# The operands of the float32r products of a Fourier and feed-forward kernel, laid out in two pools of their own at multiples of 256 bytes

## The chip, the cores and the metric

The kernel runs on one core of one Trainium2 chip. The metric is the device time of one execution in microseconds (us), median of several runs. The engines are named as in the profile: PE is TensorE's matmul, PEld its loading of weights, DVE is VectorE, ACT is ScalarE, POOL is GpSimd, SP is SyncE, which here issues DMAs.

## The reference

```python
# x: 8 x 3136 x 256 float32
X = np.fft.fft(x, axis=1); X = np.fft.fft(X, axis=2)
x = X.real.astype(np.float32)                      # real part of a 2-D Fourier transform
mu, var = mean(x, -1), mean((x - mu) ** 2, -1)
xn = (x - mu) / np.sqrt(var + 1e-06) * g_ln        # layer norm with a gain
out = x + np.maximum(xn @ w_ch1, 0.0) @ w_ch2      # 256 -> 1024 -> 256, and the residual
```

## The kernel before, in words

The transform along the sequence is done in two steps of small matrix products, with a store to a scratch tensor in DRAM and a load in another order between them (`step1`, `store1`, `relayout`, `step2`). The transform along the 256 features is folded into the first weight matrix, so that the 49 chunks of 256 tokens (`c` = 0 to 48) go from `step2` straight into the feed-forward part. Rows k and N-k of the transform are mirror images, so that one chunk stands for 512 output rows.

Nearly all work of PE is in the feed-forward part. It runs in 392 steps, `s = 8 * c + f`, where `f` is one of eight slices of 128 of the 1024 hidden features. A product of two float32 numbers is made of three float32r products, high times low, low times high and high times high (`PASSES`), so every operand exists as a pair of tiles `..._hi` and `..._lo`:

- `moe1_a(s)` (L345): six products. The weights, 128 x 128, come from `w1_hi` and `w1_lo`; the moving operand, 128 x 256, is one half (`j` = 0 or 1) of the chunk's tiles `ckl` and `ckh` (tags `ck_lo`, `ck_hi`). The two results go to a PSUM tile `ab`; ACT copies one of them (`asb`, L350), and DVE forms sum and difference in `h` (L351, L352).
- `moe1_b(s)` (L359, L360): ACT writes `h_hi` from `h` through a relu, DVE writes `h_lo`.
- `moe2(s)` (L395): twelve products. The weights are the four 128-column pieces of `h_lo` and `h_hi`, the moving operand is the slice `f` of `w2_hi` and `w2_lo`, 128 x 256; they accumulate in PSUM tiles `acc`.

`tc.manual_schedule` keeps the order in which the program issues on every engine. The main loop issues `moe1_b(s-1)`, `moe1_a(s)`, then `moe2(s-3)`; the dictionaries `late` and `after` insert the rest by step number: the next batch's transform (`fold_zw`, `fold_eo`, `fold_hi`, `fold_lo`, then `step1` with the float32r products of `t1_hi`, `t1_lo` and the tiles `fh`, `fl`, L254), `step2` (plain float32 products, L301, whose `l` part writes `ckl` on DVE at L325), the residual (plain float32 products of the tile `ck`, L419), statistics, `finish` and `store_out`. At the start the weights arrive as 64-bit floats and are turned into float32 pairs by `convert_*`, `finish_*`, `transform_w1`, `round_w1`, `split_w2`; these borrow the buffers of tags `f_hi`, `f_lo`, `h`, `h_lo`, `zw` and `s2`.

All tiles in SBUF are in two pools, `const` (one buffer each) and `work` (as many buffers as a tag's `bufs`, used in turn). Buffers follow one another in the order of first use, each at a multiple of 32 bytes, so the sizes set the addresses. The tags `ck`, `ck_hi`, `ck_lo` and `h_hi` (which `fold_zw` borrows for a tile of 2 x 264 floats) have buffers of 2112 bytes a partition, 64 bytes over a multiple of 256; `h_lo`, `f_hi` and `f_lo` have 2048. In the compiled program the starts of the float32r operands are these, modulo 256:

| operand | role | start modulo 256 |
|---|---|---|
| `w1_hi`, `w1_lo` (pieces 512 bytes apart) | weights of L345 | 224 |
| `ckh`, first half, in chunks c mod 3 = 0, 1, 2 | moving of L345 | 224, 96, 32 |
| `ckl`, first half, in chunks c mod 3 = 0, 1, 2 | moving of L345 | 160, 32, 224 |
| second half of `ckh` and `ckl` | moving of L345 | 32 more than the first |
| `w2_hi`, `w2_lo` (slices 1024 bytes apart) | moving of L395 | 224 |
| `h_lo` (pieces 512 bytes apart) | weights of L395 | 32 |
| `h_hi` in steps f mod 4 = 0, 1, 2, 3 (pieces 512 bytes apart) | weights of L395 | 96, 32, 224, 160 |
| `fh`, `fl` | moving of L254 | 32 |
| `t1_hi`, `t1_lo` | weights of L254 | 160 |

So in the steps with odd `f` the weights of L395 lie at 32 and 32, or 32 and 160; in those with even `f` at 32 and 96, or 32 and 224. The last buffer ends at byte 224,736 of a partition.

## Time and profile before

| | |
|---|---|
| median of 3 runs | 1017.01 us (1016.2 to 1017.36) |
| profiled execution, span | 1015.8 us, granted TensorE clock 1.000 |
| from that span to the median of the runs | 1.2 us |
| PE busy | 1005.0 us, 99% of the span, 8288 matmuls |
| DVE, ACT, POOL busy | 814.4, 541.2, 244.3 us |
| chain that ended last | PE 91%, of it L395 50% and L345 25% |

The profile lists no time of the profiled execution other than its span, so 1015.8 us stands beside the runs as it is; what lies around the span is at most the 1.2 us of the difference. Matmuls overlap in the array: one lasts about 280 ns in the records, and the next starts some 115 ns later. What a product costs the kernel is therefore read from the distance between starts, or from the chain, which lists a group of products with the time that it took of the chain, not from the mean duration.

### The profile page before, as it was taken

What the parts mean: (1) busy time and instruction counts of PE and PEld (TensorE: products, weight loads), DVE (VectorE), ACT (ScalarE), POOL (GpSimd) and SP (SyncE); (2) the same over time, 40 slices, a digit from 0 to 9 for tenths busy, and PEclk for the clock granted to TensorE, in tenths of its full rate; (3) what the DMA queues carried; (4) which work ended last, traced back from release to release, by engine and by line L of the source; (5) the groups of instructions that cost most, each with busy time, mean ns of one, the idle gap of its engine ahead of it and who ended that gap; (6) DMA issues with size and microseconds to landing.
All of it is one profiled execution on the core that took longest, in us unless ns stands there. A gap on an engine that the chain in (4) does not pass through costs nothing.

```text
span 1015.8 us, 21769 instructions
## 1 busy us (share of the span) xinstructions
PE 1005.0 (99%) x8288; PEld 983.7 (97%) x8289; DVE 814.4 (80%) x2190; ACT 541.2 (53%) x1416; POOL 244.3 (24%) x278
## 2 busy tenths in 40 slices
PE   9999999999999999999999999999999999999998
PEld 6799999999999999999999999999999999999998
DVE  7688887878787787878877887878788788788887
ACT  3655556554555555655556545554555554455453
POOL 2146413520153203441044301532034300000000
PEclk9999999999999999999999999999999999999999
DMA  9934243233122511333132232224101230100101
GB/s 349 262 135 136 74 148 103 84 91 107 53 94 84 156 43 53 103 118 104 44 114 95 73 105 74 83 95 134 45 32 43 73 104 23 43 22 22 43 22 43
DMA packets 41528, 92.10 MB, mean 91 GB/s; under 512 B 4176, under 2 KB 18704, under 8 KB 40528
## 3 DMA queue, kind: packets, MB, share of 16 engines
q1 hardware_dynamic: 40016, 88.87, 27.0%
q8 instruction: 66, 1.08, 0.5%
q0 software_dynamic: 320, 1.05, 0.3%
q10 hardware_dynamic: 1088, 0.79, 0.2%
q14 instruction: 38, 0.31, 0.1%
HBM read 50.32 MB, written 40.37 MB: 89 GB/s over the span
## 4 chain that ended last, share of the span: by engine, by line
PE 91%; DVE 5%; ACT 2%; DMA 1%; issue 1%; SPq 0%; DVEq 0%; ACTq 0%
PE acc L395 50%; PE ab L345 25%; PE ps L301 5%; PE psy L419 4%; PE ps L254 3%; DVE h_lo L360 2%; DVE h L351 1%; DVE h L352 1%; ACT h_hi L359 1%; PE ps L247 1%; PE ps L249 1%; PE pw L659 1%; DMA scratch<-s 1%; DMA s<-scratch 1%; ACT asb L350 0%
## 5 line engine op out<-in xcount | busy, mean ns | idle before, releaser
L395 PE MATMUL acc<-w_hi,h_hi 128*128 128x256 f32 x1568 | 438.6, 280 | 0.0
L395 PE MATMUL acc<-w_hi,h_lo 128*128 128x256 f32 x1568 | 438.4, 280 | 0.1
L395 PE MATMUL acc<-w_lo,h_hi 128*128 128x256 f32 x1568 | 438.4, 280 | 0.0
L360 DVE SCALAR_TENSOR_TENSOR h_lo<-h,h_hi 128x512 fp32r<-128x512 f32 x392 | 288.1, 735 | 168.8 <-ACT h_hi L359 166.9
L359 ACT ACTIVATE h_hi<-h 128x512 fp32r<-128x512 f32 x392 | 250.3, 639 | 266.8 <-DVE h L352 266.6
L395 PEld LDWEIGHTS acc<-w_hi,h_lo 128*128 128x128 f32 x1568 | 295.3, 188 | 0.5 <-DVE h_lo L360 0.4
L395 PEld LDWEIGHTS acc<-w_lo,h_hi 128*128 128x128 f32 x1568 | 295.0, 188 | 0.0
L395 PEld LDWEIGHTS acc<-w_hi,h_hi 128*128 128x128 f32 x1568 | 295.0, 188 | 0.0
L345 PE MATMUL ab<-ckl,w_hi 128*128 128x256 f32 x768 | 221.0, 288 | 2.7 <-DVE h L352 2.5
L345 PE MATMUL ab<-ckh,w_lo 128*128 128x256 f32 x768 | 216.2, 281 | 0.5 <-ACT ckh L321 0.3
L345 PE MATMUL ab<-ckh,w_hi 128*128 128x256 f32 x768 | 214.9, 280 | 0.0
L217 POOL TENSOR_TENSOR fl<-f,fh 128x512 fp32r<-128x512 f32 x49 | 64.7, 1321 | 502.0 <-ACT fh L211 495.7
L351 DVE TENSOR_TENSOR h<-asb,ab 128x256 f32<-128x256 f32 x384 | 158.8, 414 | 1.5 <-ACT asb L350 1.5
L352 DVE TENSOR_TENSOR h<-asb,ab 128x256 f32<-128x256 f32 x384 | 158.9, 414 | 0.0
L345 PEld LDWEIGHTS ab<-ckl,w_hi 128*128 128x128 f32 x768 | 144.5, 188 | 6.9 <-issue 2.8
L350 ACT COPY asb<-ab 128x256 f32<-128x256 f32 x384 | 139.4, 363 | 18.1 <-PE ab L345 12.5
L345 PEld LDWEIGHTS ab<-ckh,w_lo 128*128 128x128 f32 x768 | 145.0, 189 | 2.9 <-ACT ckh L321 0.5
L345 PEld LDWEIGHTS ab<-ckh,w_hi 128*128 128x128 f32 x768 | 145.1, 189 | 0.0
L321 ACT CAST ckh<-ps 128x392 fp32r<-128x392 f32 (+49 forms) x112 | 39.7, 356 | 65.5 <-PE ps L301 65.3
L257 ACT COPY s<-ps 128x508 f32<-128x508 f32 x56 | 32.7, 585 | 73.1 <-PE ps L254 60.1
L301 PE MATMUL ps<-tab_s,s 112*128 112x98 f32 (+1 forms) x512 | 65.6, 273 | 0.7 <-DMA s<-scratch 0.7
L301 PEld LDWEIGHTS ps<-tab_s,s 112*128 112x128 f32 x512 | 62.1, 192 | 1.2 <-PE pw L659 1.2
(108 smaller groups left out, 963.9 us busy)
## 6 DMA issues: line engine op xcount, KB each, us to landing
xs<-x SPq DMA_DIRECT2D x56, 512.0 KB, 4.6
out<-o SPq DMA_DIRECT2D x96, 256.0 KB, 3.1
scratch<-s SPq DMA_DIRECT2D x49, 256.0 KB, 2.2
s<-scratch SPq DMA_DIRECT2D x7, 1792.0 KB, 10.2
w1p_all<-w SPq DMA_DIRECT2D x8, 512.0 KB, 8.9
scratch<-s POOLq DMA_DIRECT2D x4, 256.0 KB, 6.4
s<-scratch SPq DMA_DIRECT2D x2, 448.0 KB, 5.8
s<-scratch SPq DMA_DIRECT2D x1, 896.0 KB, 12.3
```

The costliest lines, as they stand in the source:

```text
L217: nc.gpsimd.tensor_tensor(out=lo, in0=f, in1=hi.bitcast(F32), op=ALU.subtract)
L257: nc.scalar.copy(s[:, :, :, :127], ps[:, :, :, :127])
L301: nc.tensor.matmul(ps[:, h, k0 - base:k1 - base], s2[b][:KP, g, 128 * h:128 * h + 128], tab_s[:, h, k0:k1], start=(h == 0 and g == 2 * j), ...
L321: nc.scalar.copy(hi, src)
L345: nc.tensor.matmul(pt, wt[wi][:, j, fs], ch[xi][:, j, :w], start=(n == 0), stop=(n == 2))
L350: nc.scalar.copy(asb[:, :w], pa)
L351: nc.vector.tensor_tensor(out=h[:, :w], in0=asb[:, :w], in1=pb, op=ALU.add)
L352: nc.vector.tensor_tensor(out=h[:, w:], in0=asb[:, :m], in1=pb[:, :m], op=ALU.subtract)
L359: nc.scalar.activation(h_hi, h, AF.Relu)
L360: nc.vector.scalar_tensor_tensor(out=h_lo, in0=h, scalar=0.0, in1=h_hi.bitcast(F32), op0=ALU.max, op1=ALU.subtract)
L395: nc.tensor.matmul(acc[c, i][:, side], hs[xi][:, h0:h0 + 128], ws[wi][:, f], start=(f == 0 and side == 0 and n == 0), stop=(f == 7 and n = ...
L419: nc.tensor.matmul(ps[:, j, :129 + j], ck[:, j], ty_s[:, j, :129 + j], start=(j == 0), stop=True, skip_group_check=True)
```

## The change: two pools, and sizes that are multiples of 256 bytes

Two pools are opened ahead of `const`. `moving` holds `w2_hi`, `w2_lo`, and the tags `f_hi`, `f_lo`, `ck_hi`, `ck_lo`; an unused tile of 128 bytes at its start (`margin`) brings the first operand from byte 16,512 to 16,640, which is 65 times 256. `weights` holds `w1_hi`, `w1_lo`, `t1_hi`, `t1_lo`, and the tags `ck`, `h_hi`, `h_lo` and `s2`. The widths of `ck_hi` and `ck_lo` grow from 264 to 320 columns a half (a half is then 1280 bytes), of `ck` to 288, of `h_hi` to 576 floats (2304 bytes); the products still read the same columns. `zw` loses its unused columns. Every start in the table above becomes 0 modulo 256. Six buffers grow by 448 bytes, three by 192, four by 192, three shrink by 64, and with the margin the last buffer ends 3,968 bytes later, at 228,704. Numbers of buffers, instructions, their order on each engine and their shapes stay. Tiles that stay in `const` and `work` move to other addresses as well.

```diff
+CKW = 320
+HW = 576
...
 def tile_kernel(ctx: ExitStack, tc: tile.TileContext, x, g_ln, w1, w2, tu, tab, tz, ty, tw, out):
     nc = tc.nc
+    moving = ctx.enter_context(tc.tile_pool(name="moving", bufs=1))
+    weights = ctx.enter_context(tc.tile_pool(name="weights", bufs=1))
     const = ctx.enter_context(tc.tile_pool(name="const", bufs=1))
     work = ctx.enter_context(tc.tile_pool(name="work", bufs=2))
...
+    moving.tile([128, 32], F32, name="margin")
+    w2_hi = moving.tile([128, 8, D], F32R, name="w2_hi")
+    w2_lo = moving.tile([128, 8, D], F32R, name="w2_lo")
+    w1_hi = weights.tile([128, 2, FF], F32R, name="w1_hi")
+    w1_lo = weights.tile([128, 2, FF], F32R, name="w1_lo")
+    t1_hi = weights.tile([128, 128], F32R, name="t1_hi")
+    t1_lo = weights.tile([128, 128], F32R, name="t1_lo")
...
-    t1_hi = const.tile([128, 128], F32R, name="t1_hi")
...
-    w2_lo = const.tile([128, 8, D], F32R, name="w2_lo")
...
     def fold_zw(b, i, eng):
-        t = work.tile([128, 2, MAXW], F32, tag="h_hi" if i > 3 and b == 0 else "zw",
-                      name=f"zw{b}_{i}", bufs=4 if i > 3 and b == 0 else 3)
-        z, w = (t[:, h, :256].rearrange("p (s d) -> p s d", s=2) for h in range(2))
+        if i > 3 and b == 0:
+            t = weights.tile([128, HW], F32, tag="h_hi", name=f"zw{b}_{i}", bufs=4)
+        else:
+            t = work.tile([128, 2 * 256], F32, tag="zw", name=f"zw{b}_{i}", bufs=3)
+        z, w = (t[:, 256 * h:256 * h + 256].rearrange("p (s d) -> p s d", s=2) for h in range(2))
...
-        hi = work.tile([128, 2, 2, 128], F32R, tag="f_hi", name=f"fh{b}_{i}")
+        hi = moving.tile([128, 2, 2, 128], F32R, tag="f_hi", name=f"fh{b}_{i}", bufs=2)
...
-        lo = work.tile([128, 2, 2, 128], F32R, tag="f_lo", name=f"fl{b}_{i}")
+        lo = moving.tile([128, 2, 2, 128], F32R, tag="f_lo", name=f"fl{b}_{i}", bufs=2)
...
-            s2[b] = work.tile([128, 16, D], F32, tag="s2", name=f"s2_{b}")
+            s2[b] = weights.tile([128, 16, D], F32, tag="s2", name=f"s2_{b}", bufs=2)
...
-                chunk[c] = (work.tile([128, 2, MAXW], F32, tag="ck", name=f"ck{c}", bufs=3),
-                            work.tile([128, 2, MAXW], F32R, tag="ck_hi", name=f"ckh{c}", bufs=3),
-                            work.tile([128, 2, MAXW], F32R, tag="ck_lo", name=f"ckl{c}", bufs=3))
+                parts = (weights.tile([128, 2, CKW - 32], F32, tag="ck", name=f"ck{c}", bufs=3),
+                         moving.tile([128, 2, CKW], F32R, tag="ck_hi", name=f"ckh{c}", bufs=3),
+                         moving.tile([128, 2, CKW], F32R, tag="ck_lo", name=f"ckl{c}", bufs=3))
+                chunk[c] = tuple(p[:, :, :MAXW] for p in parts)
...
-        h_hi = work.tile([128, n], F32R, tag="h_hi", name=f"h_hi{s}", bufs=4)
-        h_lo = work.tile([128, n], F32R, tag="h_lo", name=f"h_lo{s}", bufs=4)
+        h_hi = weights.tile([128, HW], F32R, tag="h_hi", name=f"h_hi{s}", bufs=4)[:, :n]
+        h_lo = weights.tile([128, n], F32R, tag="h_lo", name=f"h_lo{s}", bufs=4)
```

In the conversion of the weights at the start, `convert_e`, `convert_m` and `w1p_all` take their buffers from the pools in which the tags now are, with the same numbers of buffers.

## The prediction, made before the changed kernel was run

> **What bounds the kernel now.** I read the page first: its summary, the share of each line in the chain, and the costliest groups.

> ```profile
> span 1015.8 us, 21769 instructions
> PE 1005.0 (99%) x8288; PEld 983.7 (97%) x8289; DVE 814.4 (80%) x2190; ACT 541.2 (53%) x1416; POOL 244.3 (24%) x278
> PEclk9999999999999999999999999999999999999999
> ...
> PE acc L395 50%; PE ab L345 25%; PE ps L301 5%; PE psy L419 4%; PE ps L254 3%; DVE h_lo L360 2%; DVE h L351 1%; DVE h L352 1%; ACT h_hi L359 1%; PE ps L247 1%; PE ps L249 1%; PE pw L659 1%; DMA scratch<-s 1%; DMA s<-scratch 1%; ACT asb L350 0%
> ...
> L395 PE MATMUL acc<-w_hi,h_hi 128*128 128x256 f32 x1568 | 438.6, 280 | 0.0
> ...
> L360 DVE SCALAR_TENSOR_TENSOR h_lo<-h,h_hi 128x512 fp32r<-128x512 f32 x392 | 288.1, 735 | 168.8 <-ACT h_hi L359 166.9
> ...
> L345 PE MATMUL ab<-ckl,w_hi 128*128 128x256 f32 x768 | 221.0, 288 | 2.7 <-DVE h L352 2.5
> ```

> PE is busy for 99% of the span at a full granted clock. Its two large lines have three passes each, of which one row stands here: 3 x 1568 = 4704 products at L395 and 3 x 768 = 2304 at L345. The last column says how long PE stood idle before them: 0.0 and 2.7 us. So the 7008 products of 256 columns set the time, and only the distance between their starts can move it: any nanosecond on each is 7.0 us. The durations of 280 ns overlap and say nothing of the distance. I took that from the chain in order of time, which merges the products of a group (start, length in us, what).

> ```profile
> 471.87 1.76 PE ps L301 x16
> 473.63 0.92 PE psy L419 x8
> 474.55 0.72 PE ab L345 x6
> 475.27 1.38 PE acc L395 x12
> 476.65 0.71 PE ab L345 x6
> 477.36 1.41 PE acc L395 x12
> 478.76 0.70 PE ab L345 x6
> 479.46 1.36 PE acc L395 x12
> 480.82 0.70 PE ab L345 x6
> 481.52 1.42 PE acc L395 x12
> 482.94 0.70 PE ab L345 x6
> 483.64 1.38 PE acc L395 x12
> 485.02 0.70 PE ab L345 x6
> 485.72 1.43 PE acc L395 x12
> ```

> The groups of twelve at L395 are the steps with f = 3, 4, 5, 6, 7, 0. The same twelve products, on the same engine with nothing to wait for, take 1.38, 1.41, 1.36, 1.42, 1.38, 1.43 us: 115, 118, 113, 118, 115, 119 ns a product. The odd steps are the short ones. What differs between odd and even steps is where `h_hi` lies: at 32 or 160 modulo 256 in the odd ones, at 96 or 224 in the even ones; `w2` is at 224 and `h_lo` at 32 in all. `moe1_a` takes 0.70 to 0.72 us for six, 117 to 120 ns. The timeline shows how the step of 1.36 us runs (start, duration); its first two products are left out.

> ```profile
> 479.52 0.28 PE L395 MATMUL acc<-w_hi,h_hi 128*128 128x256 f32 x1
> ...
> 480.54 0.28 PE L395 MATMUL acc<-w_hi,h_hi 128*128 128x256 f32 x1
> ```

> Nine distances: 1.02 / 9 = 113.3 ns, all of them 0.11 or 0.12 us in the timeline; after two or three products the distance has settled. Is it another engine that disturbs PE in the slow groups? Near the end there is a stretch with DVE and ACT idle.

> ```profile
> 1010.66 0.48 DVE L482 SCALAR_TENSOR_TENSOR o<-acc,r,y 128x256 f32<-128x256 f32 x1 [0.16 <-PE acc L395]
> ...
> 1011.03 0.28 PE L395 MATMUL acc<-w_hi,h_lo 128*128 128x256 f32 x1
> 1011.03 0.19 PEld L395 LDWEIGHTS acc<-w_lo,h_hi 128*128 128x128 f32 x1
> ...
> 1011.50 0.28 PE L395 MATMUL acc<-w_lo,h_hi 128*128 128x256 f32 x1
> ...
> 1011.58 0.48 DVE L482 SCALAR_TENSOR_TENSOR o<-acc,r,y 128x256 f32<-128x256 f32 x1 [0.43 <-PE acc L395]
> ```

> Four distances in 0.47 us are 117.5 ns, though DVE ended at 1011.14 and began again at 1011.58, and no other engine computes in between. So the slow pace is PE's own. The weight load at 1011.03 shows what runs beside each product: the loading of the next product's weights starts with it, so two streams read SBUF at once, 1024 bytes a partition moving and 512 bytes of weights. That two streams of one engine hinder each other by where they lie is my reading; the rows show only that pace goes with the address.

> **The change part by part.** Instructions, order, waits and numbers of buffers stay, so no step is moved past a queue and no wait is added. What remains are addresses.

> *Base.* From the groups above: L395 takes 1.38 in odd and 1.42 in even steps, mean 1.40 / 12 = 116.7 ns; L345 0.705 / 6 = 117.5 ns. Weighted by 4704 and 2304 that is 117.0 ns, and 7008 x 117.0 = 820 us of the 1015.8.

> *Products of 256 columns.* After the change both streams start at 0 modulo 256 in every step, which no step shows now. Ends of the bound: the shortest distance that any PE group of this kernel keeps between weight loads is L301's, 1.76 / 16 = 110 ns, in which products of only 98 columns wait for their weights; it would give 7008 x 7.0 = 49 us less. The longest group is 1.43 / 12 = 119.2 ns; everywhere it would give 7008 x 2.2 = 15 us more. Which value? In the odd steps with f mod 4 = 1 all weights lie alike (32), and the pace settles; in the even steps the two kinds of weights lie differently (32 against 96 or 224) and it stays long. The change makes all weights and all moving operands alike, in L345 too, so I take the settled pace of the step at 479.52, 113.3 ns, for nine tenths of the products and 118 for the rest (the first few after a residual or a `step2`, which are plain float32 and start the pattern anew): 0.9 x 113.3 + 0.1 x 118 = 113.8 ns. That is 7008 x 3.2 = 22.4 us less.

> [...]

> *Products of 512 columns.* L254 has 3 x 49 = 147.

> ```profile
> 420.26 0.39 PE L254 MATMUL ps<-fl,t_hi 128*128 128x512 f32 x1
> ...
> 420.96 0.28 PE L345 MATMUL ab<-ckl,w_hi 128*128 128x256 f32 x1
> ```

> From the first of three to the product that follows them, 0.70 / 3 = 233 ns each. The same ratio (113.8 / 117.0) would make it 227: 147 x 6 = 0.9 us less. Ends: 220 (110 x 2) and 238, 1.9 us less to 0.7 more.

> *Plain float32 products* (L301, L419) move too: `ck` and `s2` are now in `weights`. L301 takes 110 ns by its weight loads, L419 0.92 / 8 = 115 ns. I take zero; with 512 and 400 of them, a nanosecond is 0.9 us in all.

> *DVE, ACT, POOL.* Their tiles change addresses as well. DVE's `h_lo` takes 735 ns in the mean; DVE has 814 us of work in a span that would still be 993 us, 82%, and its work is covered by PE. If that cover went, the price is the view's own: L345 waits for L352 2.5 us now, by the last column of its row. A PE that is 2% faster shortens the slack of the three steps by which `moe2` lags `moe1_a` by 0.1 us or so; I take 0.5 us of new waits, ends 0 and 3 (the 2.5 of now once more).

> *DMA.* Destinations move, sizes do not; zero, as DMAs end few waits of PE (the chain has 2% for them).

> Sum: -22.4 - 0.9 + 0.5 = -22.8 us. Against the profiled span, 1015.8 - 22.8 = 993.0; the median of the runs lies 1.2 us above the span, so 994 us.

> **The rivals.**

> *Alignment locks in the slow pace (slower).* In the even steps `h_hi` at 96 or 224 is a multiple of 128 away from `w2` at 224, and exactly these steps are slow; in odd steps it is 64 away modulo 128, and these are fast. If what counts is that both streams start in the same place modulo 128, then the change puts every step in the slow class. Price: 118.5 ns (1.42 / 12 = 118.3, and L345 at 117 to 120) instead of 117.0, 7008 x 1.5 = 10.5 us more, 1027 us; with 119.2 everywhere 1032. It decides if the settled pace exceeds 117.0 ns. For it: the rows above. Against it: in L345 the weights are always at 224, the moving halves in chunk 21 at 224, 0, 160 and 192, in chunk 22 at 96, 128, 32 and 64, and the groups (chunk 22 from the row at 478.76 on) take 0.70 to 0.71 us in both, so the difference alone does not make the pace there. Chance 0.28.

> *Nothing low in the address matters.* The settled pace may come from higher bits or from the state in which a group begins: the step at 468.33 (f = 1, same residues as the one at 479.46) takes 1.41 us.

> ```profile
> 468.33 1.41 PE acc L395 x12
> ```

> Then the new addresses are another draw, and the mean stays at 117.0 within half a nanosecond, 3.5 us: 1013 to 1021 us, middle 1017. This is also the case in which the change does not do what it says. [...] Chance 0.22.

> *More than the settled pace.* If being aligned removes the excess altogether, PE falls to the pace of weight loads, 110 ns: 968 us; half way, 980. No step shows it. Chance 0.08, counted with the gain.

> **How the numbers follow.** Settled pace, 985 to 1008 us: 0.42, the likeliest, and its middle is the forecast, 994. Better than that, 968 to 985: 0.08. Another draw, 1013 to 1021: 0.22, of which 0.07 faster, 0.10 within, 0.05 slower. Slow lock, 1019 to 1034: 0.28, of which 0.02 within. A change of 0.2%, 2 us, is about what a measurement of this kernel can tell from none. Faster: 0.42 + 0.08 + 0.07 = 0.57; same 0.12; slower 0.05 + 0.26 = 0.31. For the range I leave out the best part of the gains (below 979) and the upper part of the slow case (above 1028): 979 to 1028. The likeliest case alone has 985 to 1008.

> **What the profile after would show.** If right: groups of twelve at L395 in the chain at 1.36 to 1.38 us in odd and even steps alike, groups of six at L345 at 0.68 to 0.69, PE still at 99%, DVE's busy time within a few us of 814. If the slow lock is right, the groups are alike but at 1.42 or more. If they still alternate or scatter from 1.36 to 1.43, low bits were not the cause. The prediction is wrong if uniform residues do not settle at 113 ns, which I have seen only at residues 32 and 160 against 224, never at 0 against 0.

## The result and the profile after

The changed kernel takes 1033.46 us (median of 4 runs, 1032.81 to 1034.1) against 1016.98 us before: 1.016 times the time, 95% interval 1.0145 to 1.0174. It is 16.5 us slower; the forecast was 994, and its range ended at 1028. The profiled execution took 1034.1 us with a span of 1032.3, 16.5 more than before.

The page of the changed kernel (lines moved: L395 is now L403, L345 is L353, L301 is L308, L419 is L427, L254 is L261):

```profile
span 1032.3 us, 21770 instructions
PE 1023.1 (99%) x8289; PEld 1002.1 (97%) x8289; DVE 812.1 (79%) x2190; ACT 545.2 (53%) x1416; POOL 243.4 (24%) x278
...
PEclk9999999999999999999999999999999999999999
...
L403 PE MATMUL acc<-w_hi,h_hi 128*128 128x256 f32 x1568 | 443.6, 283 | 0.0
...
L353 PE MATMUL ab<-ckl,w_hi 128*128 128x256 f32 x768 | 222.1, 289 | 1.7 <-DVE h L360 1.7
```

The granted clock is 1.000; DVE, ACT and POOL are busy within 4 us of what they were, and PE waits less than before (1.7 us ahead of L353 against 2.7). PE's own busy time grew by 18 us. (The one matmul more is a record of `warm_up` at the start: 20 products of `warm_h` against 19.) The chain in order of time shows where (start, length in us, what):

```profile
476.91 1.44 PE acc L403 x12
478.35 1.76 PE ps L308 x16
480.11 0.92 PE psy L427 x8
481.03 0.71 PE ab L353 x6
481.74 1.44 PE acc L403 x12
483.18 0.72 PE ab L353 x6
483.90 1.44 PE acc L403 x12
485.34 0.72 PE ab L353 x6
486.06 1.44 PE acc L403 x12
```

The alternation of before is gone: in these rows every group of twelve takes 1.44 us, every group of six 0.71 or 0.72, that is 118 to 120 ns a product. The plain float32 groups, L308 and L427, take 1.76 and 0.92 us as before. Over the trace, the time between the starts of successive products of 256 columns (those under 150 ns, 6815 of them) is 119.8 ns in the mean, and 6140 are 120 ns to the nanosecond; before, 6811 of them had 117.2 in the mean, and nearly all lay between 112 and 124. Summed over all products of the two lines, with their waits, it is 566.8 + 281.7 us against 553.6 + 278.4, 16.5 us more: the whole loss.

### The profile page after: what moved, and what is told of

Read it like the earlier page. It is cut to its first block, busy times and chain, and to the rows that moved or that the text cites. A ratio compares the mean times of both kernels' runs of the same rounds, so it can differ in the third digit from the quotient of the medians.

```text
span 1032.3 us, 21770 instructions
## 1 busy us (share of the span) xinstructions
PE 1023.1 (99%) x8289; PEld 1002.1 (97%) x8289; DVE 812.1 (79%) x2190; ACT 545.2 (53%) x1416; POOL 243.4 (24%) x278
## 4 chain that ended last, share of the span: by engine, by line
PE 91%; DVE 6%; ACT 2%; DMA 1%; issue 1%; ACTq 0%; SPq 0%; DVEq 0%
PE acc L403 50%; PE ab L353 25%; PE ps L308 5%; PE psy L427 4%; PE ps L261 3%; DVE h_lo L368 2%; DVE h L359 1%; DVE h L360 1%; ACT h_hi L367 1%; PE pw L669 1%; PE ps L254 1%; PE ps L256 1%; DMA scratch<-s 1%; DMA s<-scratch 0%; ACT asb L358 0%
## 5 line engine op out<-in xcount | busy, mean ns | idle before, releaser
L403 PE MATMUL acc<-w_hi,h_lo 128*128 128x256 f32 x1568 | 443.9, 283 | 0.1
L403 PE MATMUL acc<-w_lo,h_hi 128*128 128x256 f32 x1568 | 443.7, 283 | 0.0
L403 PE MATMUL acc<-w_hi,h_hi 128*128 128x256 f32 x1568 | 443.6, 283 | 0.0
L403 PEld LDWEIGHTS acc<-w_hi,h_lo 128*128 128x128 f32 x1568 | 300.5, 192 | 0.4 <-DVE h_lo L368 0.3
L403 PEld LDWEIGHTS acc<-w_hi,h_hi 128*128 128x128 f32 x1568 | 300.9, 192 | 0.0
L403 PEld LDWEIGHTS acc<-w_lo,h_hi 128*128 128x128 f32 x1568 | 300.9, 192 | 0.0
L353 PE MATMUL ab<-ckl,w_hi 128*128 128x256 f32 x768 | 222.1, 289 | 1.7 <-DVE h L360 1.7
L353 PE MATMUL ab<-ckh,w_lo 128*128 128x256 f32 x768 | 217.2, 283 | 0.4 <-ACT ckh L329 0.4
L353 PE MATMUL ab<-ckh,w_hi 128*128 128x256 f32 x768 | 217.0, 283 | 0.0
L359 DVE TENSOR_TENSOR h<-asb,ab 128x256 f32<-128x256 f32 x384 | 158.9, 414 | 1.5 <-ACT asb L358 1.5
L360 DVE TENSOR_TENSOR h<-asb,ab 128x256 f32<-128x256 f32 x384 | 158.8, 414 | 0.0
L353 PEld LDWEIGHTS ab<-ckl,w_hi 128*128 128x128 f32 x768 | 146.7, 191 | 5.4 <-ACT w_hi L538 1.4
L353 PEld LDWEIGHTS ab<-ckh,w_lo 128*128 128x128 f32 x768 | 146.7, 191 | 2.8 <-ACT ckh L329 0.5
L353 PEld LDWEIGHTS ab<-ckh,w_hi 128*128 128x128 f32 x768 | 146.5, 191 | 0.0
L308 PE MATMUL ps<-tab_s,s 112*128 112x98 f32 (+1 forms) x512 | 65.6, 273 | 1.1 <-DMA s<-scratch 1.1
L308 PEld LDWEIGHTS ps<-tab_s,s 112*128 112x128 f32 x512 | 62.2, 192 | 1.6 <-issue 1.6
```

The costliest lines, as they stand in the source:

```text
L308: nc.tensor.matmul(ps[:, h, k0 - base:k1 - base], s2[b][:KP, g, 128 * h:128 * h + 128], tab_s[:, h, k0:k1], start=(h == 0 and g == 2 * j), ...
L353: nc.tensor.matmul(pt, wt[wi][:, j, fs], ch[xi][:, j, :w], start=(n == 0), stop=(n == 2))
L359: nc.vector.tensor_tensor(out=h[:, :w], in0=asb[:, :w], in1=pb, op=ALU.add)
L360: nc.vector.tensor_tensor(out=h[:, w:], in0=asb[:, :m], in1=pb[:, :m], op=ALU.subtract)
L403: nc.tensor.matmul(acc[c, i][:, side], hs[xi][:, h0:h0 + 128], ws[wi][:, f], start=(f == 0 and side == 0 and n == 0), stop=(f == 7 and n = ...
```

## The experiments

Three theories could make such a uniform pace. A: what counts is the distance in bytes between the start of the moving operand and that of the weights which are loaded beside it, and at distance 0 the pace settles at its worst. B: a start at a multiple of 256 is slow in itself. C: the low bits do not matter, and the new addresses happen to be bad. In all that follows, "distance" is start of the moving operand of one product less start of the weights of the next, modulo 256.

**Moving one stream, or both.** The first kernel moves only the moving operands by 64 bytes, the second moves both:

```diff
-    moving.tile([128, 32], F32, name="margin")
+    moving.tile([128, 48], F32, name="margin")
+    weights.tile([128, 48], F32, name="margin_w")      # the first kernel only
```

> The changed kernel with every moving operand 64 bytes further on (64 modulo 256) and all weights still at 0. Theory A, the distance between the starts of the moving operand and of the weights modulo 128 sets the pace: the distance is now 64, as in the odd steps of the kernel before, so the products settle at 113.3 ns instead of 120, 7008 x 6.7 = 47 us less than the changed kernel, about 986 us. Theory B, weights that start at a multiple of 256 are slow in themselves: 120 ns stays, 1033 us. Theory C, higher address bits: the pattern is broken, mean near 117, about 1013 us.

Measured: 1020.62 us, ratio to before 1.0033 (1.0021 to 1.0044), 13 us less than the changed kernel. Its chain:

```profile
474.74 0.71 PE ab L354 x6
475.45 1.41 PE acc L404 x12
476.86 0.71 PE ab L354 x6
477.57 1.41 PE acc L404 x12
478.98 0.71 PE ab L354 x6
479.69 1.41 PE acc L404 x12
```

Again the groups are alike, but at 1.41 / 12 = 117.5 ns. Weights at multiples of 256 are not slow in themselves (B falls in this form), but theory A had the wrong number: a distance of 64 has the pace of the odd step of before that took 1.41 us (at 468.33, with a distance of 192), not the 113.3 ns that I had promised.

> The changed kernel with moving operands and weights both 64 bytes further on, so that their distance stays 0. Theory A (distance): 120 ns in all products, 1033 us. Theory B (weights, or both, at a multiple of 256 are slow in themselves): off 120, towards 113 to 117, 986 to 1015 us. Theory C: mean near 117, 1013 us.

Measured: 1033.15 us in one run, with the same groups of 1.44 and 0.72 us:

```profile
480.08 0.71 PE ab L353 x6
480.79 1.44 PE acc L403 x12
482.23 0.72 PE ab L353 x6
482.95 1.44 PE acc L403 x12
```

Both streams are off the multiples of 256, and the pace is the same 120 ns. So for this shift of 64 bytes it is the distance that counts, not the place.

**The distance swept.** Two kernels let the distance grow by 32 bytes every six chunks, by reading and writing at an offset inside the buffers (widened to 576 floats for `h_lo`, which the spare columns of `ck` pay for):

```diff
+def offset(c):
+    return 8 * min(c // 6, 7)                       # floats
...
-        h_hi = weights.tile([128, HW], F32R, tag="h_hi", name=f"h_hi{s}", bufs=4)[:, :n]
-        h_lo = weights.tile([128, n], F32R, tag="h_lo", name=f"h_lo{s}", bufs=4)
+        h_hi = weights.tile([128, HW], F32R, tag="h_hi", name=f"h_hi{s}", bufs=4)[:, o:o + n]
+        h_lo = weights.tile([128, HW], F32R, tag="h_lo", name=f"h_lo{s}", bufs=4)[:, o:o + n]
...
-                chunk[c] = tuple(p[:, :, :MAXW] for p in parts)
+                o = offset(c)                       # first sweep: -offset(c) % 64
+                chunk[c] = parts[0], parts[1][:, :, o:o + MAXW], parts[2][:, :, o:o + MAXW]
```

> The changed kernel with a distance that grows by 32 bytes every six chunks: the weights h_hi and h_lo start at d = 0, 32, ... 224 modulo 256 (w2 at 0), the moving ckh and ckl at -d (w1 at 0), so in both lines the moving operand starts d before the weights. It shows the pace against the distance in one run. Theory A: 120 ns in the first six chunks (d = 0) and about 118 to 120 at d = 128, 113.3 at d = 64 and 192, something between at the odd multiples of 32; L395 and L345 alike. Theory B: only d = 0 is slow. Theory C: 120 does not depend on d.

> As the sweep before it, but ckh and ckl start at +d: in L395 the moving operand starts d before the weights, in L345 d after them. Theory A without sign (128 periods, mirror image): both lines as in the other sweep. Theory A with a sign: L345 at d has the pace that the other sweep has at 256 - d, L395 the same as there. Theory B: L345, whose weights stay at 0, is slow in all groups.

Measured, mean time between starts in ns, some 530 products at `acc` and 230 at `ab` for each entry (the kernels took 1023.63 and 1021.59 us, one run each). The columns go by the distance as defined above: it is 256 - d, but d at `ab` in the second sweep. Only times from one product to the next of the same group are counted; between the groups one product stands at another distance (0 from `acc` to `ab` in both sweeps; from `ab` to `acc` -2d in the first, 0 in the second).

| distance, bytes | 0 | 32 | 64 | 96 | 128 | 160 | 192 | 224 |
|---|---|---|---|---|---|---|---|---|
| first sweep, `acc` | 119.9 | 117.6 | 117.9 | 119.6 | 118.6 | 117.7 | 117.4 | 118.5 |
| first sweep, `ab` | 119.6 | 117.0 | 117.7 | 119.2 | 118.1 | 118.1 | 116.9 | 118.7 |
| second sweep, `acc` | 119.9 | 116.8 | 116.1 | 119.4 | 118.7 | 118.3 | 115.9 | 118.3 |
| second sweep, `ab` | 119.6 | 117.8 | 116.4 | 120.0 | 118.3 | 117.9 | 117.0 | 118.3 |

Distance 0 is the slowest at `acc` and, with 96, at `ab`; the fastest are 64 and 192 in the second sweep, 192 and 32 in the first. `ab`, whose weights never leave their place, follows the distance too, so theories B and C fall. The sign counts: in all four rows 96 is slower than 160, by 1.1 to 2.1 ns, and 224 slower than 32, by 0.5 to 1.7. That is theory A with a sign; without a sign it falls. The period is not 128: 128 is not 0. And the pace is no function of the distance alone: at 64 and 192 the first sweep has 117 to 118 and the second 116 to 117. The chain of the second sweep, in the six chunks with offset 64, shows why:

```profile
330.35 1.37 PE acc L409 x12
331.73 0.68 PE ab L359 x6
332.41 1.42 PE acc L409 x12
333.83 0.87 PE ps L313 x8
334.69 0.92 PE psy L433 x8
335.62 0.70 PE ab L359 x6
336.32 1.38 PE acc L409 x12
337.69 0.68 PE ab L359 x6
338.38 1.42 PE acc L409 x12
```

There are two settled paces at the same addresses, 113.3 ns (0.68 for six, 1.37 for twelve, a first product of 122 included) and 117.6 (0.70, 1.42), and after its first two or three products a group keeps one of them. In these chunks the distance is 64 at `ab` and 192 at `acc`, with one product at 0 on each way between them. Counted by the last three times of a group (under or over 115.7 ns), where no other line's products lie between, the pace changes on 44 of 45 ways from `ab` to `acc` and on none of 32 from `acc` to `ab`. In the six chunks with offset 192, where `ab` has 192 and `acc` 64, it changes on none of 45 ways from `ab` to `acc` and on 30 of 32 from `acc` to `ab`. So in this run the way from 64 to 192 kicks the products from one pace to the other, and the way from 192 to 64 does not. In the kernel with 64 everywhere nothing kicks, and 763 of its 776 groups stay near 117.7 ns.

**Finer steps.** The second sweep again, in steps of 16 and of 4 bytes (`4 *` and `1 *` in `offset`).

> As the second sweep, in steps of 16 bytes: d = 0, 16, ... 112 for six chunks each. In the sweeps by 32 bytes only 0, 64 and 192 settled; 64 and 192 in two paces, 113.3 and 117.6. Theory A1 (the distance counts in units of 64 bytes, the rest is noise of the phase): 16 and 48 scatter like 32 and 96, 116 to 120 in the mean. Theory A2 (a finer distance selects the pace): one of 48 or 80 settles at 113.3 alone, another at 117.6.

> As the second sweep, in steps of 4 bytes: d = 0, 4, ... 28 for six chunks each. Theory A1 (lines of 64 or 32 bytes decide): the pace leaves 120 as soon as d is not 0, and scatters between 116 and 120 with the same mean for all d from 4 to 28. [...]

Measured (1024.04 and 1023.54 us, one run each): at `acc`, offsets of 0, 16, 32, 48, 64, 80, 96, 112 gave 119.9, 118.1, 118.3, 118.1, 116.0, 118.7, 118.3, 120.1 ns; offsets of 0, 4, ... 28 gave 119.9, 118.0, 116.4, 117.4, 118.1, 119.2, 119.9, 117.1. The same offset gives the same value in another run: 32, 64 and 96 have 118.3, 115.9 and 118.3 in the second sweep, and 16 has 118.1 in both finer ones. So 120 is left at once when the offset is not 0, but there is no single value after that (A1 of the steps of 4 falls; for 16 and 48 it holds), 24 and 112 are back at 120, 16 does not settle as 0 does (118.1 against 119.9), and the pace neither falls nor rises step by step, nor does 48 or 80 settle at 113.3 (118.1 and 118.7, A2 falls). Every part of the distance counts, down to 4 bytes. I have no formula for it.

**Less weight data.** If the stream of weights hinders the moving stream, half the weights should cost less:

```diff
-                nc.tensor.matmul(acc[c, i][:, side], hs[xi][:, h0:h0 + 128], ws[wi][:, f],
+                k = 64 if f and n < 2 else 128
+                nc.tensor.matmul(acc[c, i][:k, side], hs[xi][:, h0:h0 + k], ws[wi][:, f],
```

> The changed kernel (distance 0), but in L395, in steps with f > 0, two of the three products of a piece load and use only the first 64 of 128 weight columns, so the loading of weights that runs beside a product reads half as much before two of three products; half of these two terms is left out of the result. Theory A (the weight stream hinders the moving stream): a product beside a half load is shorter than 120 ns, at most 113, one beside a full load stays at 117 to 120; with about 2744 products 7 to 10 ns shorter some 20 to 27 us less than the changed kernel, 1006 to 1013 us. Rival D (the moving stream is slow by itself when it starts at a multiple of 256, whatever is loaded beside it): 120 ns everywhere, 1033 us.

Measured: 1021.12 us, 12 us less than the changed kernel. The timeline (start, duration) of the three products of one piece and the one after them, the shape 128*64 being the half, and of the loads that start beside the three:

```profile
499.97 0.28 PE L404 MATMUL acc<-w_hi,h_lo 128*64 128x256 f32 x1
500.09 0.28 PE L404 MATMUL acc<-w_lo,h_hi 128*64 128x256 f32 x1
500.21 0.28 PE L404 MATMUL acc<-w_hi,h_hi 128*128 128x256 f32 x1
500.32 0.28 PE L404 MATMUL acc<-w_hi,h_lo 128*64 128x256 f32 x1
...
499.98 0.13 PEld L404 LDWEIGHTS acc<-w_lo,h_hi 128*64 128x64 f32 x1
500.09 0.19 PEld L404 LDWEIGHTS acc<-w_hi,h_hi 128*128 128x128 f32 x1
500.21 0.13 PEld L404 LDWEIGHTS acc<-w_hi,h_lo 128*64 128x64 f32 x1
```

0.35 / 3 = 117 ns. So of the three, the first is a half product beside a half load, the second a half product beside a full load, the third a full product beside a half load. Over the run, in the steps with f > 0, they take 116.2, 117.4 and 117.4 ns; in the steps with f = 0, where nothing was halved, 119.6 to 120.0. Same moving operands at the same places, so rival D, the moving stream alone, falls. But the gain is half of what I expected, neither kind beside a half load comes to the 113 ns of theory A, and the pace does not go with the load: products beside a full load became faster as well, and a full product beside a half load is no faster than they are. The settled state is broken as a whole. That the weights' reading is what hinders the moving stream is not shown by this run; half products also write half as many rows of the result, which it does not separate either.

**Choosing the kicks.** One kernel tries eight choices of where `h_hi`, `h_lo`, `ckh` and `ckl` start, six chunks each, by four offsets in place of one.

> The changed kernel with w1 and w2 at 0 and eight choices, six chunks each, of where h_hi, h_lo, ckh and ckl start modulo 256 (bytes): (192,64,64,192), (192,64,192,64), (64,192,64,192), (64,192,192,64), (192,64,64,64), (64,192,64,64), (192,64,192,192), and last (8,8,28,28). At a distance of 64 or 192 in all products the kernel settles at 117.6 (the run with moving operands at 64), where the distance changes between products or groups at 113.3 in part (second sweep, 116.0 in the mean at L395). Theory A with a kick (a change of distance shifts the phase, and 113.3 is reached only after it): the first seven have means between 113.5 and 117, those with the higher parts at one distance and the lower at the other, as in the odd steps f = 3 and 7 of the kernel before, the lowest. Rival F (the distance alone sets the pace, 64 and 192 are alike): all seven at 117.6 in the mean. The last choice: 115 to 117 without settling.

Measured: 1016.77 us in one run; the eight choices have, over `acc` and `ab` together, 117.3, 117.3, 118.1, 117.2, 116.8, 115.5, 115.9 and 115.8 ns. The rival (117.6 in all seven) falls by the three at 115.5 to 116.8. But theory A had all seven below 117, and four are at 117.2 to 118.1. Its order falls too: `h_hi` and `h_lo` lie apart in all seven, and the three fastest are those in which `ckh` and `ckl` start alike, the fifth to the seventh. The sixth and the last were then run alone, in all chunks, together with a kernel that puts the distances of before back into the changed layout:

```diff
+        n, o = 2 * CW, (32, 16, 0, 48)[s % 4]                     # h_hi; h_lo at 16 floats
...
+                at = (0, 32, 16)[c % 3], (48, 16, 0)[c % 3]        # ckh, ckl, halves 264 floats apart
```

> The changed kernel, pools and sizes as they are, but every product of L345 and L395 reads its operands at offsets inside their buffers that give back the distance modulo 256 that the kernel before had, product by product (h_hi by s mod 4, ckh and ckl by c mod 3); absolute places, pools and everything else stay as changed. Theory A (the distance between moving operand and next weights, modulo 256, is the whole effect): the pattern of 113 to 122 ns of before comes back, mean 117.2, and the time of before, 1017 us, within 2. Rival G (something else in the change, such as higher address bits or the other tiles that moved, costs part of the 16 us): between 1020 and 1033 us.

Measured: 1017.16 us, ratio to before 1.0001 (0.9992 to 1.0011). The chain, for the same steps as those shown of before:

```profile
474.59 1.37 PE acc L405 x12
475.96 0.71 PE ab L355 x6
476.67 1.41 PE acc L405 x12
478.07 0.70 PE ab L355 x6
478.77 1.36 PE acc L405 x12
480.13 0.70 PE ab L355 x6
480.83 1.42 PE acc L405 x12
482.25 0.70 PE ab L355 x6
482.95 1.38 PE acc L405 x12
484.33 0.70 PE ab L355 x6
485.03 1.43 PE acc L405 x12
```

1.37, 1.41, 1.36, 1.42, 1.38, 1.43: the groups of before, one by one, each within 0.01 us, with all pools, sizes and higher bits those of the change. Over the run, 354 of 392 groups at `acc` and 325 of 384 at `ab` have a mean within 1 ns of before, and the mean of all is 117.2 ns again. Rival G and theory C fall: the distances modulo 256 are the whole effect on the time, to within 0.1%.

> The changed kernel with h_hi at 64, h_lo at 192, ckh and ckl at 64 in all chunks, the sixth choice of the run with eight, which had 115.5 ns a product there. Theory A: it keeps that, 7008 x (119.8 - 115.5) = 30 us less than the changed kernel and 7008 x (117.2 - 115.5) = 12 us less than the kernel before, 1003 to 1008 us. Rival (the state at the start of each six chunks made the difference): 1010 to 1020 us.

Measured: 1004.94 us, ratio to before 0.9877 (0.9864 to 0.9891), 12 us faster than before and 28.5 faster than the change.

```profile
span 1003.4 us, 21769 instructions
PE 992.7 (99%) x8288; PEld 971.6 (97%) x8289; DVE 812.4 (81%) x2190; ACT 539.5 (54%) x1416; POOL 244.0 (24%) x278
...
478.08 1.38 PE acc L403 x12
479.46 0.68 PE ab L353 x6
480.14 1.39 PE acc L403 x12
481.53 0.68 PE ab L353 x6
```

In these rows `ab` is in the fast pace, 0.68 / 6 = 113 ns, and `acc` at 115 to 116. Over the run, 269 of 384 groups at `ab` are near 114 ns and 104 near 118, so it is not fast everywhere; the mean of both lines is 115.5 as in the trial.

> The changed kernel with h_hi and h_lo at 8 and ckh and ckl at 28, the last choice of that run, which had 115.8 ns there, unsettled. Theory A: 7008 x (117.2 - 115.8) = 10 us less than before, 1005 to 1010 us. Rival (the state at the start made the difference): 1010 to 1020 us.

Measured: 1009.44 us, ratio to before 0.9929 (0.9916 to 0.9941). Both beat the kernel before, and differ from the changed kernel only in offsets inside the buffers and the widths that hold them.

## Why the prediction was wrong

- *What bounds the kernel:* right. All of the 16.5 us lies in the 7008 products of 256 columns; the busy times of DVE, ACT and POOL moved by -2.3, +4.0 and -0.9 us, which PE's work covers, and there were no new waits (I had 0.5 us; it was 1 less).
- *Another engine does not cause it, the two streams of PE do, by where they lie:* right as a reading; the old distances in the new layout give back the old time, and in the stretch shown the old groups to within 0.01 us. What hinders what inside PE stays open.
- *One settled pace for uniform addresses:* right. 382 of the 392 groups at L403 and 272 of the 384 at L353 are at 120 ns, alike as "what the profile after would show" asked.
- *Which pace:* this step failed. I took 113.3 ns from the step at 479.52, that is from a distance of 192, and carried it over to distance 0. The argument was that being alike is what settles the pace. Being alike settles it, but the distance sets where: 120 ns at 0, 117.5 at 64 alone. The term was -22.4 us by 113.8 ns; by 119.8 ns it is 7008 x 2.6 = +18 us on the measured 117.2. The tenth at 118 ns, for products after plain float32 ones, was an estimate that the changed kernel does not bear out: the groups that follow L427 take 0.71 and 1.44 us there, as the others do. The two lines grew by 16.5, as the times before a wait or another line's product became shorter.
- *The sample behind 113.3:* the step at 479.52 has f = 5 in chunk 21. The steps with f = 5 of the next two chunks are these:

```profile
498.08 1.38 PE acc L395 x12
...
517.66 1.42 PE acc L395 x12
```

Over the trace of before, f = 5 has 113.4 ns a product in chunks with c mod 3 = 0, as in chunk 21, 114.8 with 1 and 117.4 with 2. Its own weights lie alike in all of them; what changes with c mod 3 is where the chunk's tiles lie, and with them the `ab` products ahead of the group. All steps with weights at one place (f = 1 and 5) have 115.6 in the mean, and f = 7, with weights at two places, 114.6. So 113.3 was the fastest of three cases, and lying alike was not what made it fast.

- *The slower rival* had the right mechanism (the same place modulo a power of two locks in the slow pace) at 28%, though its 128 was wrong (118.1 to 118.7 ns at 128 in the sweeps, 119.6 to 119.9 at 0), and its price of 118.5 ns was too low; the ceiling of 119.2 from which I priced it, and cut the range, was itself too low by 0.6 to 0.8 ns. Its case "with 119.2 everywhere 1032" came within 1.5 us, in part by luck (0.6 ns too little is 4 us, but the base was 0.2 ns too low and the other times became shorter), and I left it out of the range. Against it I had held that `ab` showed the same 0.70 to 0.71 us in two chunks at several distances: but a group of six there has four distances (0, 32, 192 and 224 in chunk 21), so it was no evidence on the settled pace of one distance.
- *The row that I had and did not weigh:* the step at 468.33, with the residues of the one at 479.46 and 1.41 us in place of 1.36, already showed two settled paces at one distance. I filed it under "nothing low matters", of which the part on the state at the start of a group holds and the part on higher bits falls. It meant that 113.3 is not given even where it exists.
- *That the pace goes with the address:* the runs show it more clearly than the trace of before did, 120 ns at distance 0 against 113 to 117.6 at 64 with the same instructions; among starts that are all multiples of 32 the settled paces differ by 7 ns a product. Whether the loading of weights takes anything from the running product, no run here shows.
- *Products of 512 columns:* I had 227 ns, they took 232.6 against 230.8 before, 0.3 us in all. *Plain float32 products:* zero was right, 1.76 us for sixteen and 0.92 for eight in all kernels.

## What to carry to other kernels

Where PE runs float32r products back to back, read the time between starts, not the busy share: 99% busy held from 1003 to 1032 us of span here. Do not align the moving operand and the weights alike (120 ns a product here); give them different starts (a mix of 64 and 192 bytes gave 1004.94 us here, 64 everywhere 1020.62, which is slower than before), and measure, since the pace that a stretch settles in depended here on how it was entered (0.68 or 0.70 us for six products at one distance of 64 in the second sweep). Other widths than 256 columns and other types were not tried. A short offset inside a buffer is enough for the trial, and several choices can be tried in one run, a few chunks each.
